# A new token order for the attention quads with an output piece, two DMAs for the rows of maxima, and a second bias that stays in its tile

## The chip, the cores and the metric

The kernel runs on one core of a Trainium2 chip. The metric is device time of one launch in microseconds, here the median of three runs. A profile is one further execution under the hardware profiler, with times of its own.

## The reference

One transformer block on a 2048 x 576 input, all in fp32. A modulation vector comes from silu(c) @ w_mod and gives shifts (sa, sb), scales (ca, cb) and gates (ga, gb). Attention has 32 query heads of width 18 over one shared key and value head; the MLP has 4608 hidden columns.

```python
x = A_x
h = layernorm(x) * (1 + ca) + sa
q = (h @ wq)  # 32 heads of 18
k, v = h @ wk, h @ wv  # one head of 18
p = softmax(q k^T / sqrt(18))
x = x + ga * ((p v) @ wo)
h = layernorm(x) * (1 + cb) + sb
y = layernorm(h)
x = x + gb * (gelu(y @ w1 + b1) @ w2 + b2)
```

## The kernel before

**Stages.** First come the norm, the projections of q, k and v, and the maxima of the first quad. Then attention, which the change is about, and last the MLP, in 36 steps (18 column groups for each half of the rows).

**Attention in quads.** A quad `n` is four heads and one block of 512 rows: 4 blocks x 8 quads = 32 quads (0 to 31). Matmuls of the scores contract over 64 rows of the array: two heads side by side in row group 0 and two in row group 1. A query tile `qst` holds for each group the split query and, in two more rows (`R3`), the negated maximum of every query row, so that the score matmul subtracts it. So the maxima of quad n+1 have to be found while quad n runs.

**The order written out by hand.** PE's work in a quad is a string of tokens (lines 884 to 896), and the loop at line 982 goes through it: `QUAD` for quads 0 to 8, `QUADW` for quads 9 to 30, `LAST` for quad 31. The tokens:

- `S0`, `S1` (`st_mm`, line 928): scores of 128 keys against 512 queries in row group 0 or 1, into one of four `psB` buffers; ACT writes the exponential to `P` (line 934). 64 a quad.
- `M0`, `M1` and `R1` (`mx_mm`, line 938): scores of 128 queries against 512 keys in row group 0 or 1, into one of three `psM` buffers; DVE takes the maximum along each row (line 954). For `R1` it is joined with the result of an earlier `X1` (line 952). `X1` goes through `psB` and is evicted by ACT (line 945). Together 64 a quad.
- `V2`, `V3`, `V4` (`pv_mm`, line 915): so many units of P times V into the single `psC`, 64 units a quad, 8 units behind the scores: the first 8 units in quad n belong to quad n-1. A key block is 4 units. At each full key block, `between` (line 956) puts a step of other work into the queues: at odd ones a step of `fill` (the layer norm of finished output tiles), and from quad 4 on one or two steps of `prep` (splitting and storing the MLP's weights, on POOL, with DMAs on SP's queue), except at the three key blocks in `quiet`.
- `T1`, `RC`, `T2`, `OS`: the steps of `post_quad` (line 733) for quad n-1. ACT copies `psC` to `O` as soon as its last unit is done (line 738); `T1` is a DVE transpose (741), `RC` a DVE reciprocal and a POOL product (744, 745), `T2` a DVE transpose (747), `OS` an ACT copy, a POOL difference and four DMAs (757, 758, 762). There is one `O`.
- `F1`, `F2` (`smax_fin1`, `smax_fin2`, lines 347 and 355): F1 reduces the maxima of quad n+1 on DVE; F2 transposes them on PE (357), ACT and DVE negate and split them into `ms` (359, 360), and SP's queue sends them to the query tile (364).
- `WO` (line 971): one output piece, a 128-row tile by 288 columns of P V @ wo for an earlier block, 14 matmuls into a `psB`, added to the rows by DVE (727). There is one in each quad of `QUADW`. Behind the second piece of a tile in the first two blocks, which falls in the even quads 10 to 24, the layer norm of that tile is put into `fill` (`ln2_rows`, `ln2_tile`): statistics on DVE (143, 147, 148), the norm on POOL (585, 599, 600), statistics again, the norm again, the second bias added (617); its transposes on PE follow the WO two quads later.

An engine runs its own instructions in the order of the program and waits where an operand or a buffer is not ready. A matmul's wait for a PSUM buffer shows at its weight load (PEld).

**The second bias.** `load_b2` and `b2_scaled` (lines 625 and 630) load b2 to all partitions and scale it on POOL by the gate and by 2. This is done once in attention and once more at the start of the MLP, since the tile's pool is closed in between (lines 1100 and 1409).

Of the kernel before, what the change touches and what calls it, by code (L numbers as in the profile page):

```python
# [8 lines left out]
F32 = mybir.dt.float32  # L9
# [15 lines left out]
R3 = 3 * DH  # L25
# [7 lines left out]
def block_kernel(ctx: ExitStack, tc, x, wqkv, wo, w1, b1, w2, b2, c, wmod, ident_in, out):  # L33
# [94 lines left out]
    QST = {}  # L128
# [226 lines left out]
    def smax_fin2(n):  # L355
        p = psB()
        pe.transpose(p[:16, :128], MR.pop(n), ident)  # L357
        ms = pa.tile([16, 2, 128], F32R, name="ms")
        ac.activation(ms[:, 0], p[:16, :128], AF.Copy, scale=-1.0)
        ve.scalar_tensor_tensor(ms[:, 1], p[:16, :128], -1.0, ms[:, 0].bitcast(F32), op0=ALU.mult, op1=ALU.subtract)  # L360
        for g in range(2):
            for s in range(2):
                r = 64 * g + R3 + s
                sy.dma_start(QST[n][r:r + 1].rearrange("o p (t c) -> o (p t) c", c=128).bitcast(F32),
                             ms[8 * g:8 * (g + 1), s].bitcast(F32))


    for t in range(NT):
# [254 lines left out]
        yield  # L623

    def load_b2():
        b2g = px.tile([128, D], F32, name="b2g")
        sy.dma_start(b2g, b2.to_broadcast([128, D]))
        return b2g

# [103 lines left out]
    def post_quad(n, PV):  # L733

        tb, qd = divmod(n, NQ)
        e = po if n < NQT - 1 else ve
        O = px.tile([128, TB], F32, name="O")
        ac.activation(O, PV, AF.Copy)
        yield
        T = px.tile([128, 16, 32], F32, name="T")  # L740
        ve.transpose(T.rearrange("p a b -> p (a b)"), O)
        yield
        R = px.tile([128, 16], F32, name="R", bufs=2)
        ve.reciprocal(R, T[:, :, DH])
        e.tensor_tensor(T, T, R[:, :, None].to_broadcast([128, 16, 32]), op=ALU.mult)
        yield
        ve.transpose(O, T.rearrange("p a b -> p (a b)"))
        yield
        if tb not in ATT:
            assert tb  # L750
            ATT[tb] = big()
        A = ATT[tb].rearrange("p (s k) t -> p s k t", s=2)
        if n == NQT - 1:
            os = A[:, :, KD - 1, :]
        else:
            os = px.tile([128, 2, TB], F32R, name="os")
        ac.activation(os[:, 0], O, AF.Copy)  # L757
        e.tensor_tensor(os[:, 1], O, os[:, 0].bitcast(F32), op=ALU.subtract)  # L758
# [125 lines left out]
    QUAD = """S0 M0 S1 S1 M0 V3 S0 M1 S1 M0 M1 S0 V3 M0 S1 M1 S0 V2 M0 S1 S1 M0 X1 S0 V4 T1 X1 M0 M1 M0 S1 S0
            V4 S1 RC M0 S1 S0 M0 S0 M1 V3 S0 M1 R1 S1 S0 M0 X1 V3 M0 S1 S1 R1 S0 M0 S1 V3 M0 X1 M0 S0 S1 S0
            M1 V3 M0 S1 S1 M0 S0 R1 S0 V3 R1 S0 S1 M1 S0 M0 X1 V3 M0 S1 M0 S1 S0 S0 R1 V3 M0 X1 S0 M1 S0 M1
            V3 S1 M0 M0 S1 T2 S0 S1 V4 M0 S1 S0 M1 S0 M1 V3 S0 R1 S1 M0 F1 S1 S0 V3 X1 M0 S1 M0 R1 S0 F2 OS
            V4 M0 M1 S0 S1 M0 X1 V4 S1 M0 S1 S0 M1 M0 S1 V2 R1 S0 M1 S0 V2 S0 S1 M0 M1 V2 S1""".split()
    QUADW = """M1 M1 S0 S0 X1 S1 M0 V4 S1 M0 S1 S0 M1 M0 V4 M0 S1 S0 M0 S1 T1 M0 X1 V4 S1 RC S0 S0 M1 M0 S1 V4
            S0 R1 M1 S0 S1 M0 S1 V3 S1 M0 S0 X1 M0 M0 S1 V2 M0 S1 S0 R1 V2 M0 X1 M0 S1 S0 S1 M0 V4 S0 T2 R1  # L890
            M0 S1 OS S0 M1 WO S0 R1 M1 S0 M1 S0 X1 V3 S0 M1 M0 S1 S1 M1 S0 V3 M0 S1 S0 R1 S0 M0 X1 V3 M0 S1
            X1 M0 S1 M0 S1 V4 S1 M0 R1 S0 M1 S0 V4 S0 M1 M0 F1 S1 S0 S1 V4 M0 S1 M0 X1 S0 M1 F2 V4 M1 S0 S0
            S1 M0 S1 M0 V3 R1 S0 S0 S1 R1 M0 V3 S0 S1 M0 S1 M0 S1 V3 M0 S1 M1 S0 M1 S0 V3""".split()
    LAST = """S1 S0 S1 S0 V8 S1 S0 T1 S1 S0 RC S1 S0 WO S0 S1 S0 T2 S1 V5 S1 S0 S1 S0 S1 OS S0 V11 S0 S1 S0 S1 S0
            S1 WO RW S1 S0 S0 S1 S0 S1 V8 S0 S1 S0 S1 S0 S1 V8 S1 S0 S1 S0 S0 S1 WP S0 S1 S0 S1 V8 S0 S1 S0 S1
            S0 S1 V8 S0 S1 S0 S1 S0 S1 WP S0 S1 S0 S1 V12""".split()
# [85 lines left out]
    for n in range(NQT):  # L982
# [367 lines left out]
    for v in range(NV):  # L1350
# [158 lines left out]
```

## Time and profile before

| | us |
|---|---|
| median of 3 runs (2224.18 to 2224.81) | 2224.63 |
| the profiled execution | 2227.88 |
| its span, first to last instruction | 2225.8 |
| PE busy | 2204.6 |
| DVE busy | 1931.1 |
| ACT busy | 1639.8 |
| POOL busy | 1524.9 |
| from one F2 transpose to the next, QUADW | 39.3 to 39.9 |

A row of the profile names line and engine, the operation, the tile written and the tiles read, the shapes, the count, then busy time and the mean of one instruction, then the engine's idle time ahead of them and what ended it. A row of a timeline has the start in us from the span's beginning, the time that the merged instructions took from the first start to the last end, engine, line, operation, tiles and count; in brackets the idle time before it. A row of the windows has a stretch, its length, and the busy time (with the count of instructions) of PE, PEld, DVE, ACT and POOL, then the granted clock, the DMA share and GB/s. The granted TensorE clock was 0.997 of full speed over the span. Matmuls overlap in the rows, so starts are more telling than durations.

### The profile page before, as it was taken

What the parts mean: (1) busy time and instruction counts of PE and PEld (TensorE: products, weight loads), DVE (VectorE), ACT (ScalarE), POOL (GpSimd) and SP (SyncE); (2) the same over time, 40 slices, a digit from 0 to 9 for tenths busy, and PEclk for the clock granted to TensorE, in tenths of its full rate; (3) what the DMA queues carried; (4) which work ended last, traced back from release to release, by engine and by line L of the source; (5) the groups of instructions that cost most, each with busy time, mean ns of one, the idle gap of its engine ahead of it and who ended that gap; (6) DMA issues with size and microseconds to landing.
All of it is one profiled execution on the core that took longest, in us unless ns stands there. A gap on an engine that the chain in (4) does not pass through costs nothing.

```text
span 2225.8 us, 46116 instructions
## 1 busy us (share of the span) xinstructions
PE 2204.6 (99%) x16638; PEld 1450.8 (65%) x16638; DVE 1931.1 (87%) x3417; ACT 1639.8 (74%) x3145; POOL 1524.9 (69%) x1761
## 2 busy tenths in 40 slices
PE   8999999999999999999999999999999999999999
PEld 6654545454544545445454446888888898989898
DVE  7589999999999999999999983887888878888887
ACT  5569999999999999999999998544444444343443
POOL 6654356666776687677676640988888867877776
PEclk9999999999999999999999999999999999999999
DMA  6242143343333332333333322666666646676664
GB/s 228 85 133 93 34 128 122 127 137 109 125 121 123 115 129 94 114 130 111 115 121 118 125 70 69 200 179 174 178 179 181 185 129 182 180 218 188 177 184 124
DMA packets 184776, 308.00 MB, mean 138 GB/s; under 512 B 19711, under 2 KB 75407, under 8 KB 184549
## 3 DMA queue, kind: packets, MB, share of 16 engines
q1 hardware_dynamic: 184405, 304.91, 44.2%
q8 instruction: 132, 2.16, 0.4%
q14 instruction: 95, 0.78, 0.1%
q10 hardware_dynamic: 144, 0.15, 0.0%
HBM read 200.97 MB, written 93.79 MB: 132 GB/s over the span
## 4 chain that ended last, share of the span: by engine, by line
PE 92%; ACT 1%; DVE 1%; POOL 0%; issue 0%; DMA 0%; ACTq 0%; POOLq 0%; DVEq 0%
PE psC L922 23%; PE psB L1147 18%; PE psA L1250 16%; PE psB L932 14%; PE psM L319 12%; PE psB L723 2%; PE psB L942 2%; PE psA L1284 1%; ACT P L934 1%; PE psA L723 0%; PE psB L155 0%; PE psB L248 0%; PE psB L357 0%; DVE mx L344 0%; DVE mx L337 0%
## 5 line engine op out<-in xcount | busy, mean ns | idle before, releaser
L934 ACT ACTIVATE P<-psB 128x512 f32<-128x512 f32 x2013 | 1055.0, 620 | 42.7 <-PE psM L319 19.4
L954 DVE TENSOR_REDUCE mx<-psM 128x1 f32<-128x512 f32 x1476 | 934.2, 682 | 30.7 <-PE psM L319 16.0
L932 PE MATMUL psB<-qst,KS 64*128 64x512 f32 x2013 | 606.3, 434 | 0.1
L319 PE MATMUL psM<-KS,qst 64*128 64x512 f32 x1722 | 591.5, 435 | 0.6 <-DVE mx L337 0.5
L922 PE MATMUL psC<-P,V 128*32 128x256 f32 (+3 forms) x6608 | 569.0, 440 | 0.0
L932 PEld LDWEIGHTS psB<-qst,KS 64*128 64x128 f32 x2013 | 302.6, 184 | 218.3 <-ACT P L934 185.5
L319 PEld LDWEIGHTS psM<-KS,qst 64*128 64x128 f32 x1722 | 284.0, 184 | 186.1 <-DVE mx L954 130.5
L1147 PE MATMUL psB<-ops,w1a 128*128 128x512 f32 x1512 | 393.8, 396 | 0.2 <-DVE h L1162 0.2
L1147 PEld LDWEIGHTS psB<-ops,w1a 128*128 128x128 f32 x1512 | 270.1, 188 | 46.6 <-DVE h L1162 0.6
L922 PEld LDWEIGHTS psC<-P,V 128*32 128x32 f32 x6608 | 147.0, 108 | 187.9 <-issue 160.4
L1256 DVE TENSOR_TENSOR XT<-psA,XT 128x576 f32<-128x576 f32 x330 | 241.7, 753 | 20.1 <-PE psA L1250 14.7
L1250 PEld LDWEIGHTS psA<-w2s,big 128*128 128x128 f32 x1584 | 222.9, 188 | 15.5 <-POOL big L1224 3.6
L1250 PE MATMUL psA<-w2s,big 128*128 128x288 f32 x1584 | 230.8, 295 | 0.9 <-POOL big L1224 0.8
L1160 ACT ACTIVATE psB<-gs 128x512 f32<-128x512 f32 x144 | 86.7, 602 | 127.9 <-DVE gs L1159 127.8
L1224 POOL TENSOR_TENSOR big<-s,big 128x512 fp32r<-128x512 f32 x132 | 170.9, 1295 | 10.6
L952 DVE CUSTOM_DVE_ANT_0 xc<-psM,xc 128x512 f32<-128x512 f32 x246 | 166.3, 682 | 12.7 <-PE psB L932 4.5
L1156 ACT ACTIVATE h<-psB,b1t 128x512 f32<-128x512 f32 x144 | 97.9, 680 | 102.0 <-PE psB L1147 79.7
L945 ACT ACTIVATE xc<-psB 128x512 f32<-128x512 f32 x246 | 154.6, 628 | 4.2 <-PE psM L319 1.5
L758 POOL TENSOR_TENSOR os<-O,os 128x512 fp32r<-128x512 f32 x31 | 39.9, 1286 | 171.3 <-ACT os L757 171.3
L1159 DVE SCALAR_TENSOR_TENSOR gs<-psB,h 128x512 f32<-128x512 f32 x144 | 98.5, 684 | 38.5 <-ACT psB L1157 38.3
L792 POOL TENSOR_TENSOR r<-r,r 128x256 fp32r<-128x256 f32 (+1 forms) x162 | 121.8, 752 | 13.0
L1165 ACT ACTIVATE big<-h 128x512 fp32r<-128x512 f32 x39 | 24.7, 633 | 133.8 <-DVE h L1162 133.8
(212 smaller groups left out, 3325.2 us busy)
## 6 DMA issues: line engine op xcount, KB each, us to landing
w1a<-w1scr SPq DMA_DIRECT2D x252, 256.0 KB
w2s<-w2sum SPq DMA_DIRECT2D x132, 288.0 KB
w1scr<-r SPq DMA_DIRECT2D x126, 256.0 KB
w2s<-w2scr SPq DMA_DIRECT2D x76, 288.0 KB
w2scr<-r SPq DMA_DIRECT2D x72, 288.0 KB
w2sum<-r SPq DMA_DIRECT2D x72, 288.0 KB
qst<-qscr SPq DMA_DIRECT2D x192, 72.0 KB
w1a<-w2scr SPq DMA_DIRECT2D x33, 288.0 KB
```

The source lines that it names most:

```text
L319: pe.matmul(o, QST[n][64 * g:64 * g + 64, p, 128 * qt:128 * (qt + 1)], KS[64 * g:64 * g + 64, 512 * kb:512 * (kb + 1)], start=True, stop=True)
L792: po.tensor_tensor(o[:, n:2 * n], src, o[:, :n].bitcast(F32), op=ALU.subtract)
L922: pe.matmul(PVt[n][32 * j:32 * (j + 1), cs], V[:, kc, :], t[:, j, cs], start=(kc == 0 and h0 == 0), stop=(kc == 15), skip_group_check=True)
L932: pe.matmul(t, KS[64 * g:64 * g + 64, 128 * kc:128 * (kc + 1)], QST[n][64 * g:64 * g + 64, i, :], start=True, stop=True)
L934: ac.activation(P[n, kc][:, 2 * i + g, :], t, AF.Exp, scale=SCALE)
L945: ac.activation(XC[-1], t, AF.Relu)
L952: ve.tensor_tensor_reduce(c, t, c, 1.0, -3.0e38, ALU.add, ALU.max, o)
L954: ve.tensor_reduce(o, t, axis=AX.X, op=ALU.max)
L1147: pe.matmul(o, x, y, start=(first and i == 0), stop=(i == len(terms) - 1), skip_group_check=True)
L1224: po.tensor_tensor(unit(u, 1), x, unit(u, 0).bitcast(F32), op=ALU.subtract)
L1250: pe.matmul(p[:, i, :288], x[:, ts_], W2S[k][:, y], start=(bool(first) and q == 0), stop=(q == 2), skip_group_check=True)
L1256: ve.tensor_tensor(o, p[:, :, :288], o, op=ALU.add)
```

## The change

Five edits. `QUAD` is only wrapped anew, its tokens are the same. `QUADW` has the same kinds and numbers of tokens for scores, maxima and steps in another order; the 64 units of P V are cut into one V2, ten V3 and eight V4 in place of two, eight and nine; T1 stands behind unit 19 (was 8), RC behind 28 (12), T2 and WO behind 34 (27), OS behind 61 (27), F1 and F2 both behind 52 (44 and 48). The key blocks in `quiet` follow from the places of F2 and RC; they are 6, 11 and 12 in QUADW (were 2, 10 and 11). The rows of maxima go out in two DMAs of 16 rows rather than four of 8. The second bias has a tile that lives to the end, so the second load and the second scaling go. `post_quad` may step `fill` for the first block's tile, which is there by then anyway.

```diff
-        for g in range(2):
-            for s in range(2):
-                r = 64 * g + R3 + s
-                sy.dma_start(QST[n][r:r + 1].rearrange("o p (t c) -> o (p t) c", c=128).bitcast(F32),
-                             ms[8 * g:8 * (g + 1), s].bitcast(F32))
+        for s in range(2):
+            r = R3 + s
+            sy.dma_start(QST[n][r:r + 65:64].rearrange("g p (t c) -> g (p t) c", c=128).bitcast(F32),
+                         ms[:, s].bitcast(F32))
...
-        b2g = px.tile([128, D], F32, name="b2g")
+        b2g = per.tile([128, D], F32, name="b2g")
...
         if tb not in ATT:
-            assert tb
-            ATT[tb] = big()
+            while not tb and tb not in ATT:
+                step(fill)
+            if tb not in ATT:
+                ATT[tb] = big()
...
-    QUADW = """M1 M1 S0 S0 X1 S1 M0 V4 S1 M0 S1 S0 M1 M0 V4 M0 S1 S0 M0 S1 T1 M0 X1 V4 S1 RC S0 S0 M1 M0 S1 V4
-            S0 R1 M1 S0 S1 M0 S1 V3 S1 M0 S0 X1 M0 M0 S1 V2 M0 S1 S0 R1 V2 M0 X1 M0 S1 S0 S1 M0 V4 S0 T2 R1
-            M0 S1 OS S0 M1 WO S0 R1 M1 S0 M1 S0 X1 V3 S0 M1 M0 S1 S1 M1 S0 V3 M0 S1 S0 R1 S0 M0 X1 V3 M0 S1
-            X1 M0 S1 M0 S1 V4 S1 M0 R1 S0 M1 S0 V4 S0 M1 M0 F1 S1 S0 S1 V4 M0 S1 M0 X1 S0 M1 F2 V4 M1 S0 S0
-            S1 M0 S1 M0 V3 R1 S0 S0 S1 R1 M0 V3 S0 S1 M0 S1 M0 S1 V3 M0 S1 M1 S0 M1 S0 V3""".split()
+    QUADW = """M1 X1 S0 S1 M0 S0 R1 V4 M0 S1 M0 X1 S1 M0 V4 S0 M1 M0 S1 S0 S1 M0 V4 S0 M1 S0 S1 M0 X1 M0 V4 S0 M1
+            M0 S1 S0 S1 M0 V3 R1 S0 S1 R1 S0 M0 T1 S1 V4 S0 S1 M0 M1 M0 S1 V2 X1 S0 S1 M0 V3 RC M0 S1 S0 M1 S0
+            M1 V3 S1 S0 M0 M1 S0 S1 V3 M0 S1 S1 M0 S0 T2 R1 WO X1 M0 M1 M0 X1 S0 S1 V3 R1 S0 S0 M1 S1 M1 S0 V4
+            S0 M1 X1 M0 S1 S0 V3 R1 M0 S1 S0 S1 M0 V4 M0 S1 S0 R1 S0 S1 M0 V4 X1 F1 M0 S1 M0 M1 S0 F2 V3 S1 M0
+            S1 M0 S0 R1 S0 V3 M1 S0 M1 S0 S1 M0 S1 V3 M1 S0 S1 M0 M0 S1 OS V3""".split()
...
-            kf, kr = (sum(int(tok[1]) for tok in order[:order.index(a)] if tok[0] == "V") // 4 for a in ("F2", "RC"))
+            kf, kr = (sum(int(tok[1:]) for tok in order[:order.index(a)] if tok[0] == "V") // 4 for a in ("F2", "RC"))
...
-    B2["b"] = load_b2()
...
-        if v == 0:
-            b2_scaled(B2["b"])
```

More of the change, by code (lines that the diff above doesn't have):

```diff
@@ L883, in block_kernel @@
     LAG = 8
[L884 to L888, printed above, removed]
-    QUADW = """M1 M1 S0 S0 X1 S1 M0 V4 S1 M0 S1 S0 M1 M0 V4 M0 S1 S0 M0 S1 T1 M0 X1 V4 S1 RC S0 S0 M1 M0 S1 V4
-            S0 R1 M1 S0 S1 M0 S1 V3 S1 M0 S0 X1 M0 M0 S1 V2 M0 S1 S0 R1 V2 M0 X1 M0 S1 S0 S1 M0 V4 S0 T2 R1
-            M0 S1 OS S0 M1 WO S0 R1 M1 S0 M1 S0 X1 V3 S0 M1 M0 S1 S1 M1 S0 V3 M0 S1 S0 R1 S0 M0 X1 V3 M0 S1
-            X1 M0 S1 M0 S1 V4 S1 M0 R1 S0 M1 S0 V4 S0 M1 M0 F1 S1 S0 S1 V4 M0 S1 M0 X1 S0 M1 F2 V4 M1 S0 S0
-            S1 M0 S1 M0 V3 R1 S0 S0 S1 R1 M0 V3 S0 S1 M0 S1 M0 S1 V3 M0 S1 M1 S0 M1 S0 V3""".split()
+    QUAD = """S0 M0 S1 S1 M0 V3 S0 M1 S1 M0 M1 S0 V3 M0 S1 M1 S0 V2 M0 S1 S1 M0 X1 S0 V4 T1 X1 M0 M1 M0 S1 S0 V4
+            S1 RC M0 S1 S0 M0 S0 M1 V3 S0 M1 R1 S1 S0 M0 X1 V3 M0 S1 S1 R1 S0 M0 S1 V3 M0 X1 M0 S0 S1 S0 M1 V3
+            M0 S1 S1 M0 S0 R1 S0 V3 R1 S0 S1 M1 S0 M0 X1 V3 M0 S1 M0 S1 S0 S0 R1 V3 M0 X1 S0 M1 S0 M1 V3 S1 M0
+            M0 S1 T2 S0 S1 V4 M0 S1 S0 M1 S0 M1 V3 S0 R1 S1 M0 F1 S1 S0 V3 X1 M0 S1 M0 R1 S0 F2 OS V4 M0 M1 S0
+            S1 M0 X1 V4 S1 M0 S1 S0 M1 M0 S1 V2 R1 S0 M1 S0 V2 S0 S1 M0 M1 V2 S1""".split()
+    QUADW = """M1 X1 S0 S1 M0 S0 R1 V4 M0 S1 M0 X1 S1 M0 V4 S0 M1 M0 S1 S0 S1 M0 V4 S0 M1 S0 S1 M0 X1 M0 V4 S0 M1
[3 more added lines that the diff above has]
+            S1 M0 S0 R1 S0 V3 M1 S0 M1 S0 S1 M0 S1 V3 M1 S0 S1 M0 M0 S1 OS V3""".split()
     LAST = """S1 S0 S1 S0 V8 S1 S0 T1 S1 S0 RC S1 S0 WO S0 S1 S0 T2 S1 V5 S1 S0 S1 S0 S1 OS S0 V11 S0 S1 S0 S1 S0
```

## The prediction

> **What bounds the kernel now.** I read the page first, then the timelines of TensorE (PE), VectorE (DVE), ScalarE (ACT), GpSimd (POOL) and of the DMA queue over single quads, then the windows from one maxima transpose to the next. In the page, see that PE is busy all the time and carries the chain, while its weight loads for the scores stand idle until an ACT or DVE instruction has freed a PSUM buffer.
>
> ```profile
> span 2225.8 us, 46116 instructions
> PE 2204.6 (99%) x16638; PEld 1450.8 (65%) x16638; DVE 1931.1 (87%) x3417; ACT 1639.8 (74%) x3145; POOL 1524.9 (69%) x1761
> PE 92%; ACT 1%; DVE 1%; POOL 0%; issue 0%; DMA 0%; ACTq 0%; POOLq 0%; DVEq 0%
> ...
> L934 ACT ACTIVATE P<-psB 128x512 f32<-128x512 f32 x2013 | 1055.0, 620 | 42.7 <-PE psM L319 19.4
> L954 DVE TENSOR_REDUCE mx<-psM 128x1 f32<-128x512 f32 x1476 | 934.2, 682 | 30.7 <-PE psM L319 16.0
> ...
> L932 PEld LDWEIGHTS psB<-qst,KS 64*128 64x128 f32 x2013 | 302.6, 184 | 218.3 <-ACT P L934 185.5
> ```
>
> The profiled execution took 2227.88 us for its span of 2225.8, 3.25 over the median of 2224.63; the terms below are differences, so I add them to the median.
>
> QUADW rules quads 9 to 30. Quad 30 has no maxima left, so 21 quads count. Their time on PE, by rows (starts are subtracted):
>
> ```profile
> 794.49 0.50 PE L932 MATMUL psB<-qst,KS 64*128 64x512 f32 x2
> ...
> 795.62 1.06 PE L922 MATMUL psC<-P,V 128*32 128x512 f32 x8
> ```
> ```profile
> 808.59 0.50 PE L932 MATMUL psB<-qst,KS 64*128 64x512 f32 x1
> ...
> 809.71 0.86 PE L922 MATMUL psC<-P,V 128*32 128x256 f32 x16
> 810.50 0.50 PE L319 MATMUL psM<-KS,qst 64*128 64x512 f32 x1
> ...
> 820.50 0.49 PE L319 MATMUL psM<-KS,qst 64*128 64x512 f32 x1
> ...
> 821.63 0.85 PE L922 MATMUL psC<-P,V 128*32 128x384 f32 x7
> ```
> ```profile
> 858.19 0.50 PE L319 MATMUL psM<-KS,qst 64*128 64x512 f32 x1
> ...
> 859.09 0.28 PE L357 MATMUL psB<-ident,mxf 128*16 128x128 f32 x1
> 859.29 1.07 PE L922 MATMUL psC<-P,V 128*32 128x512 f32 x8
> 860.29 0.49 PE L319 MATMUL psM<-KS,qst 64*128 64x512 f32 x1
> ...
> 861.50 0.85 PE L922 MATMUL psC<-P,V 128*32 128x384 f32 x8
> ...
> 867.72 0.47 PE L932 MATMUL psB<-qst,KS 64*128 64x512 f32 x1
> ```
>
> Call a run of score and maxima tokens with the V behind it a period. A token of row group 0 and one of row group 1 run together and take one slot; two of one group in a row take two. Three slots took 0.90 us (858.19 to 859.09), four 1.12 (808.59 to 809.71), so 0.22 a slot and 0.68 for two; V3 took 0.79 (809.71 to 810.50), V4 1.00 (859.29 to 860.29), so V2 0.58; the transpose of F2 0.20. A run that takes more than its slots has waited for PSUM: the old fourth period (S1 RC S0 S0 M1 M0 S1, three slots) took 1.13, so 0.23 was lost.
>
> **The change part by part. PE's own work: 0.** Slots by period, old: 4 3 4 3 4 4 2 4 7 4 4 4 3 3 3 4 3 3 3; new: 4 3 4 4 4 4 3 2 3 3 7 4 3 3 4 3 4 4 3 (7 is the run that WO splits into 3 and 4). Both sums are 69, both orders have 19 V with 64 units, and both split one run at WO. What can move is only what PE waits, so I keep a ledger for ACT and for DVE: what a period hands an engine, less the period's length on PE, carried on and never under zero.
>
> **ACT: 0.20 us a quad gained.**
>
> ```profile
> 793.07 1.57 ACT L934 ACTIVATE P<-psB 128x512 f32<-128x512 f32 x3
> 794.50 0.63 ACT L945 ACTIVATE xc<-psB 128x512 f32<-128x512 f32 x1
> ```
>
> Three evictions follow each other in 1.43 us: 0.48 each. The copy of O comes in the third period of both orders; with four evictions that is 2.40 against 2.12, 0.28 behind. Old, the fourth period adds 1.92 against 1.90, and there the 0.23 is lost. New, the fourth is S0 M1 S0 S1 M0 X1 M0: 1.92 against 2.12, and the ledger falls to 0.08. I take 0.20 of the 0.23; the bounds are 0 and 0.23.
>
> **DVE: the new peaks are higher.**
>
> ```profile
> 795.32 0.23 DVE L744 RECIPROCAL R<-T 128x16 f32<-128x16 f32 x1
> ...
> 802.09 1.88 DVE L954 TENSOR_REDUCE mx<-psM 128x1 f32<-128x512 f32 x3
> 803.89 0.45 DVE L147 BATCH_NORM_STATS2 bst<-Z 128x6 f32<-128x288 f32 x1
> 804.38 0.21 DVE L148 BATCH_NORM_AGGREGATE mv<-bst 128x2 f32<-128x12 f32 x1
> 804.50 0.66 DVE L747 STREAM_TRANSPOSE O<-T 128x512 f32<-128x512 f32 x1
> ...
> 818.40 0.19 DVE L352 TENSOR_REDUCE mxf<-mx 128x8 f32<-128x32 f32 x1
> ...
> 820.74 0.27 DVE L360 SCALAR_TENSOR_TENSOR ms<-psB,ms 16x128 fp32r<-16x128 f32 x1
> ```
>
> A maximum costs 0.60 (three from 802.09 to 803.89); R1 I take alike, T1 and T2 0.66 each. F1 has two reductions, by the first 0.19 at most each and partly overlapped: 0.27; F2 0.27. The layer norm of an output tile, which runs in every other pair of quads behind a WO, has statistics of 0.45 and then of 0.61 (803.89 to 804.50).
>
> How much backlog is free, the old order shows. In an even quad the second statistics fall into its 15th period: three maxima, F2 and 0.61 are 2.68 against 0.90+0.20+1.00, a backlog of 0.58, and the run behind it took 1.21 (860.29 to 861.50); in the odd quad without them the same run took 1.13 (820.50 to 821.63). So 0.58 cost 0.08: I count what goes over 0.50, one for one, as lost.
>
> New, in every quad T1 meets two R1 and a maximum (sixth period, R1 S0 S1 R1 S0 M0 T1 S1 V4): 2.46 against 2.12, +0.34; next S0 S1 M0 M1 M0 S1 with only V2 behind it: 1.80 against 1.48. Backlog 0.66, lost 0.16.
>
> In even quads (10, 12 to 24, eight of them) WO stands at unit 34 and no longer at 27, so the statistics come one odd key block later. The first (0.45) fall into the 15th period: 2.25 against 2.12, 0.13. The 16th now holds F1 and F2 together with a V3: 2.34 against 1.89, 0.58. The 17th gives back 0.11; the 18th carries the second statistics: 2.41 against 1.91, 0.97; the 19th: 1.80 against 1.69, 1.08. Over 0.50: 0.58 lost. In the odd quads behind them (eight) that remainder is gone after five periods; the statistics of the normed tile bring the ninth period to about 0.58: 0.08 lost.
>
> **POOL: RC and T2 come close together.**
>
> ```profile
> 799.00 1.05 POOL L745 TENSOR_TENSOR T<-T,R 128x512 f32<-128x512 f32 x1
> ...
> 807.55 1.28 POOL L758 TENSOR_TENSOR os<-O,os 128x512 fp32r<-128x512 f32 x1
> ...
> 828.65 1.95 POOL L135 MEMSET qst<- 32x1024 f32 x2
> ...
> 862.69 2.30 POOL L585 TENSOR_SCALAR Z<-XT,mv,rs 128x576 f32<-128x576 f32 x1
> 865.07 1.42 POOL L599 TENSOR_TENSOR Z<-Z,BC 128x576 f32<-128x576 f32 x1
> ```
> ```profile
> 898.45:938.27 39.82, 39.82 (x350) 19.93 (x348) 37.89 (x76) 37.83 (x77) 23.57 (x34) 1.00 0.34 113
> 938.27:977.66 39.39, 39.39 (x345) 19.06 (x344) 37.99 (x75) 37.33 (x76) 32.78 (x44) 1.00 0.35 114
> ```
>
> The reciprocal of RC ended at 795.55 and POOL's product began at 799.00, 3.45 late, but T2 came at 804.50, so 4.45 were to spare. New, RC stands at unit 28 and T2 at 34: 0.90+0.79+0.90+0.79+0.90 = 4.28, less 0.23 and 1.05, leave POOL 3.0 of lateness. What it has to do since OS, now at unit 61: 1.28, in odd quads the norm (2.30+1.42, and L600 estimated like L599: 5.14), the clearing of a quad's buffer 1.95, and 12 preparation steps at about 0.84 ((23.57-1.05-1.28-1.95)/23, 23 steps a quad in both orders): 18.5, begun 0.6 behind OS (ACT's copy), against 0.79 and eight periods, 16.0. So it is about 3.1 late, just what is free. DVE waits at T2, with R1 and WO's addition queued behind; PE sees it only after the output piece. Bounds 0 and 1.5 an odd quad, the upper one if its waits for stores fall there; I take 0.25, near the computed 0.1.
>
> OS itself moves with a copy on ACT, 1.28 on POOL and four DMAs on SP. Behind them stand preparation stores and the next query loads, which nothing needs within the quad; the rows of maxima are issued before them. The next copy of O, 0.79+2.12+1.90 later, hides POOL's part. Cost 0; if POOL were behind there, ACT would hold psC.
>
> **Two DMAs: 0.**
>
> ```profile
> 860.48 2.84 SPq L364 DMA_DIRECT2D qst<-ms  x4
> ```
>
> Four issues took 2.84 and ended 4.40 before the next quad's first score (867.72). New, that score is 0.20+6.30+0.3 = 6.8 behind F2 and the issues begin 1.39 behind it and take 1.42, or 2.84 if the price goes by rows: 4.0 or 2.6 are left for landing. If landing needs more, every quad pays the rest.
>
> **Second bias: 1.0 us gained, once.**
>
> ```profile
> 1397.95 1.43 POOL L631 TENSOR_TENSOR b2g<-b2g,BC 128x576 f32<-128x576 f32 x1
> 1399.47 1.67 POOL L632 TENSOR_SCALAR b2g<-b2g 128x576 f32<-128x576 f32 x1
> ```
> ```profile
> 1403.33 3.06 PE L1147 MATMUL psB<-ops,w1a 128*128 128x512 f32 x12 [0.19 <-DVE h L1162]
> ...
> 1408.35 1.59 PE L1250 MATMUL psA<-w2s,big 128*128 128x288 f32 x10 [0.81 <-POOL big L1224]
> ```
>
> POOL's two products go, 3.1 us on the way to the GELU sums for which PE waits 0.81, then 0.19 for DVE. Next late would be DVE's h. Bounds 0 and 1.0 in seen waits; I take 1.0. The reload's DMA goes too, off the chain.
>
> **Sum.** Quads 9 and 26 to 29: 5 x (0.16-0.20) = -0.2. Odd: 8 x (0.16+0.08+0.25-0.20) = 2.3. Even: 8 x (0.16+0.58-0.20) = 4.3. Less 1.0: +5.4, so 2230.0 us.
>
> **The rivals. Faster.** PE's three psM buffers may swallow a backlog of 1.0 when it grows over several periods; then the DVE terms fall away and ACT's whole 0.23 is won: 21 x 0.23 + 1.0 = 5.8, 2218.8 us. For it: the loss that a row shows is ACT's. Against it: 1.21 against 1.13 came at a backlog of 0.58. It decides if the runs of the 7th and 19th periods keep 0.90.
>
> **No difference.** PE's waits have one cause in both orders, four psB and three psM buffers, and only the bias pays: 2223.6 us. For it: 218.3 us of idle weight loads spread over all quads. Against it: 1.21 and 1.13 differ with the same buffers. The Trainium skill, Perfetto Trace Analysis, Optimization Strategy, says that the same gap repeating on the engine that should be saturated can mean too few PSUM buffers; by that rule the order alone gives nothing.
>
> **Slower yet.** POOL's stores push its lateness in odd quads to the upper bound, and T2 costs 1.5: 8 x 1.25 more, 2240.0 us. For it: 3.45 late already. Against it: WO covers. A late landing of the maxima I hold for 3 in 100.
>
> **How the numbers follow.** About 0.2%, 4.4 us, is what a measurement here can tell from no change. The forecast's ledger has 0.50: its terms give +1 to +10, of which 0.36 lies over 0.2% and 0.14 under. Faster 0.20, no difference 0.13, slower yet 0.14, landing 0.03. So faster 0.20, same 0.27, slower 0.53. The range 2218 to 2240 ends at the outer rivals.
>
> **What would show it.** Right: unchanged V times, the new fourth run at 1.12, the run before V2 (0.90 bare) and the last runs of even quads longer than their slots, T2 straight behind POOL's product in odd quads. Wrong: quads of 39.3 and 39.9 us or less in place of more, or a first score that waits for a DMA.

## The result and the profile after

The changed kernel takes 2243.84 us (median of 5 runs, 2242.39 to 2245.43), the kernel before, run beside it, 2224.63 (5 runs, 2223.74 to 2227.01). The ratio is 1.0086, with an interval of 1.0074 to 1.0097: 19.2 us slower, where 5.4 were forecast and the range ended at 2240. The profiled execution took 2242.97 for its span of 2241.2.

The page of the kernel after; its lines L935, L955 and L933 are L934, L954 and L932 of before.

```profile
span 2241.2 us, 46379 instructions
PE 2210.4 (99%) x16814; PEld 1457.2 (65%) x16814; DVE 1929.6 (86%) x3417; ACT 1643.0 (73%) x3145; POOL 1523.7 (68%) x1759
PE 87%; DVE 5%; POOL 4%; ACT 1%; issue 1%; DMA 1%; SPq 0%; POOLq 0%; ACTq 0%; DVEq 0%
...
L319 PE MATMUL psM<-KS,qst 64*128 64x512 f32 x1722 | 588.0, 441 | 11.5 <-DVE mx L953 9.9
...
L933 PEld LDWEIGHTS psB<-qst,KS 64*128 64x128 f32 x2013 | 309.1, 185 | 174.3 <-ACT P L935 125.6
L319 PEld LDWEIGHTS psM<-KS,qst 64*128 64x128 f32 x1722 | 272.0, 185 | 209.1 <-DVE mx L955 150.8
```

The busy times hardly moved. The chain did: PE's share fell from 92% to 87%, DVE's rose from 1% to 5% and POOL's from 0% to 4%. The idle weight loads of the scores fell from 218.3 to 174.3 us, so ACT holds PE less; those of the maxima rose from 186.1 to 209.1, so DVE holds it more. And a wait is new: that of L319 as PE itself, not as weight load, idle 9.9 us for DVE at L953, which is R1's maximum.

The windows of the kernel after, one for each quad, from first token to first token: quads 10 to 17, then quad 27. The columns are length, PE, PEld, DVE, ACT, POOL, granted clock, DMA share, GB/s.

```profile
506.97:546.77 39.80, 39.69 (x355) 19.80 (x352) 37.78 (x76) 37.76 (x77) 23.56 (x33) 1.00 0.35 114
546.77:592.28 45.51, 42.36 (x355) 19.99 (x352) 37.66 (x75) 37.24 (x75) 37.66 (x48) 0.92 0.31 105
592.28:632.67 40.39, 40.27 (x361) 20.48 (x357) 38.12 (x77) 38.35 (x78) 21.42 (x33) 1.00 0.34 109
632.67:673.60 40.93, 39.80 (x355) 19.18 (x351) 37.66 (x75) 37.28 (x75) 33.30 (x43) 1.00 0.36 124
673.60:713.99 40.39, 40.27 (x360) 20.50 (x356) 38.09 (x77) 38.34 (x78) 25.17 (x37) 1.00 0.30 98
713.99:753.47 39.48, 39.48 (x355) 19.30 (x351) 37.58 (x75) 37.11 (x75) 35.78 (x47) 1.00 0.39 134
753.47:793.84 40.37, 40.26 (x360) 20.48 (x356) 38.09 (x77) 38.31 (x78) 20.36 (x31) 1.00 0.32 105
793.84:836.11 42.27, 39.84 (x355) 19.22 (x351) 37.68 (x75) 37.29 (x75) 35.75 (x45) 1.00 0.36 118
...
1201.09:1240.23 39.14, 39.14 (x355) 19.50 (x351) 37.06 (x73) 37.36 (x76) 25.41 (x37) 1.00 0.34 113
```

Read three kinds of quads. Quad 27, without a norm, takes 39.14 (39.25 before). The even quads 12 to 24 take 40.38, each like the other (39.91 before), and quad 10, the first, 39.80 (39.36). The odd quads 11 to 25 took 39.27 before, all alike within 0.04; now no two neighbours agree: 45.51, 40.93, 39.48, 42.27, 40.69, 39.49, 43.67 and 39.92, on average 41.50. In quads 11, 13 and 17 PE is busy 1.1 to 3.2 us less than the quad is long, and in quad 11 the granted clock is 0.92. POOL is far busier in odd quads than in even ones, 33 to 38 us against 20 to 25.

The sum of it: quads 9 to 30 took 867.35 us and now take 888.24, so 20.9 more. Eight odd quads give 8 x 2.23 = 17.8 of that, the even ones 3.7, the others -0.7. From quad 31 to the end it was 886.30 and is 885.72. The spans of the two profiles differ by only 15.4, because the profiled execution of before took 4.9 us more ahead of quad 9, where its clock was at half once more (from 48.9 to 52.3). The change has no part in that: the version with the new order alone, up to there the same kernel as before, also took some 4 us less.

Where PE stands in quad 11, in PE's timeline of the kernel after:

```profile
566.76 2.12 PE L722 MATMUL psB<-wos,big 126*128 126x288 f32 x14
568.80 0.50 PE L943 MATMUL psB<-KD,qst 64*128 64x512 f32 x1
568.81 0.72 PE L319 MATMUL psM<-KS,qst 64*128 64x512 f32 x2
572.68 0.79 PE L319 MATMUL psM<-KS,qst 64*128 64x512 f32 x1 [3.15 <-DVE mx L953]
```

After the output piece PE gets two more maxima in and stops: all three psM buffers are full. It waits for R1's buffer, and DVE's and POOL's timelines say why R1 is late.

```profile
562.76 0.24 DVE L743 RECIPROCAL R<-T 128x16 f32<-128x16 f32 x1
...
571.33 0.71 DVE L746 STREAM_TRANSPOSE O<-T 128x512 f32<-128x512 f32 x1 [3.40 <-POOL T L744]
571.96 0.65 DVE L953 CUSTOM_DVE_ANT_0 xc<-psM,xc 128x512 f32<-128x512 f32 x1
```
```profile
543.85 0.23 POOL L149 TENSOR_SCALAR rs<-mv 128x1 f32<-128x1 f32 x1 [10.66 <-DVE mv L148]
...
548.76 1.30 POOL L759 TENSOR_TENSOR os<-O,os 128x512 fp32r<-128x512 f32 x1
550.05 2.31 POOL L584 TENSOR_SCALAR Z<-XT,mv,rs 128x576 f32<-128x576 f32 x1
...
557.39 1.94 POOL L135 MEMSET qst<- 32x1024 f32 x2
...
564.09 1.42 POOL L830 TENSOR_TENSOR w2b<-w2b,BC 128x576 f32<-128x576 f32 x1
...
570.24 1.05 POOL L744 TENSOR_TENSOR T<-T,R 128x512 f32<-128x512 f32 x1
```

The reciprocal ended at 563.00 and POOL's product began at 570.24, 7.2 late, because POOL was still at the work queued ahead of it. T2 waits for the product, and R1 stands behind T2 on DVE. Over the whole execution DVE's wait at T2 comes to 11.2 us in five quads, at most 3.4; the kernel before has no such wait:

```profile
DVE O L746 <- POOL T L744: 11.2, 5, 3.4
```

By the rows of the reciprocal and the product the product is late in quads 11, 13, ... 25 by 7.25, 5.21, 3.50, 6.53, 4.94, 3.58, 6.45 and 3.50. Quads 15 and 21 with about 3.5 are the shortest; above that the quad grows almost one for one: quad 13's product is 1.7 later than quad 15's and the quad takes 1.5 more, quad 17's is 3.0 later and the quad takes 2.8 more. Quad 25, also 3.50 late, takes 39.92, which the lateness does not explain: DVE does not wait at T2 there, but a score's weight load behind the output piece waits 0.51 us for ACT's eviction of an X1, which it does not in quad 21.

### The profile page after: what moved, and what is told of

Its sections match the earlier page's. It is cut to its first block, busy times and chain, and to the rows that moved or that the text cites. A ratio compares the mean times of both kernels' runs of the same rounds, so it can differ in the third digit from the quotient of the medians.

```text
span 2241.2 us, 46379 instructions
## 1 busy us (share of the span) xinstructions
PE 2210.4 (99%) x16814; PEld 1457.2 (65%) x16814; DVE 1929.6 (86%) x3417; ACT 1643.0 (73%) x3145; POOL 1523.7 (68%) x1759
## 4 chain that ended last, share of the span: by engine, by line
PE 87%; DVE 5%; POOL 4%; ACT 1%; issue 1%; DMA 1%; SPq 0%; POOLq 0%; ACTq 0%; DVEq 0%
PE psC L923 20%; PE psB L1147 18%; PE psA L1250 16%; PE psM L319 11%; PE psB L933 11%; PE psB L248 2%; DVE mx L955 2%; PE psB L722 2%; PE psB L943 2%; PE psA L1284 1%; DVE xc L953 1%; POOL r L793 1%; PE psB L155 1%; PE psA L319 1%; PE psA L722 1%
## 5 line engine op out<-in xcount | busy, mean ns | idle before, releaser
L935 ACT ACTIVATE P<-psB 128x512 f32<-128x512 f32 x2013 | 1046.0, 616 | 30.6 <-PE psB L933 12.7
L955 DVE TENSOR_REDUCE mx<-psM 128x1 f32<-128x512 f32 x1476 | 932.1, 682 | 38.0 <-PE psM L319 21.6
L319 PE MATMUL psM<-KS,qst 64*128 64x512 f32 x1722 | 588.0, 441 | 11.5 <-DVE mx L953 9.9
L933 PE MATMUL psB<-qst,KS 64*128 64x512 f32 x2013 | 592.8, 433 | 0.4 <-ACT xc L946 0.2
L923 PE MATMUL psC<-P,V 128*32 128x384 f32 (+3 forms) x6784 | 571.0, 434 | 0.0
L933 PEld LDWEIGHTS psB<-qst,KS 64*128 64x128 f32 x2013 | 309.1, 185 | 174.3 <-ACT P L935 125.6
L319 PEld LDWEIGHTS psM<-KS,qst 64*128 64x128 f32 x1722 | 272.0, 185 | 209.1 <-DVE mx L955 150.8
L923 PEld LDWEIGHTS psC<-P,V 128*32 128x32 f32 x6784 | 153.2, 109 | 195.8 <-issue 167.8
L953 DVE CUSTOM_DVE_ANT_0 xc<-psM,xc 128x512 f32<-128x512 f32 x246 | 166.0, 682 | 20.9 <-PE psM L319 11.8
```

Source lines behind the costliest of these rows:

```text
L319: pe.matmul(o, QST[n][64 * g:64 * g + 64, p, 128 * qt:128 * (qt + 1)], KS[64 * g:64 * g + 64, 512 * kb:512 * (kb + 1)], start=True, stop=True)
L923: pe.matmul(PVt[n][32 * j:32 * (j + 1), cs], V[:, kc, :], t[:, j, cs], start=(kc == 0 and h0 == 0), stop=(kc == 15), skip_group_check=True)
L933: pe.matmul(t, KS[64 * g:64 * g + 64, 128 * kc:128 * (kc + 1)], QST[n][64 * g:64 * g + 64, i, :], start=True, stop=True)
L935: ac.activation(P[n, kc][:, 2 * i + g, :], t, AF.Exp, scale=SCALE)
L953: ve.tensor_tensor_reduce(c, t, c, 1.0, -3.0e38, ALU.add, ALU.max, o)
L955: ve.tensor_reduce(o, t, axis=AX.X, op=ALU.max)
```

## The experiments

**The order alone: the kernel before with the new QUADW and nothing else.**

```diff
-    QUADW = """M1 M1 S0 S0 X1 S1 M0 V4 S1 M0 ...
+    QUADW = """M1 X1 S0 S1 M0 S0 R1 V4 M0 S1 ...
```

> The kernel before with the new QUADW alone (four DMAs for the maxima, the second load of the bias kept). Theory A (the order costs it all, through POOL's late product in odd quads): 19 to 21 us over before, about 2245; odd quads 11 to 25 between 39.5 and 45.5 us as in the changed kernel, even ones 12 to 24 at 40.4. Rival B (the two wider DMAs or the longer-lived bias tile take a part): clearly less, 2230 to 2238.

2246.27 us, ratio 1.010 (1.0085 to 1.0116); odd quads 41.24 on average, even 40.44, light ones 39.16. The whole loss is the order's, and it falls on the odd quads with the same pattern (44.42, 40.94, 39.48, 43.73, ...).

**The rest alone: the kernel after with the old QUADW,** so two DMAs and the bias tile.

```diff
-    QUADW = """M1 X1 S0 S1 M0 S0 R1 V4 M0 S1 ...
+    QUADW = """M1 M1 S0 S0 X1 S1 M0 V4 S1 M0 ...
```

> The changed kernel with the old QUADW put back, so only the two DMAs and the bias tile are left of the change. Theory A (the order costs it all): the quads as before (39.27 odd, 39.91 even), the stretch behind attention 0.6 to 1.0 us shorter for the bias, 2223 to 2224.5. Rival B (the two DMAs or the bias tile cost something that the order's loss hid): 2226 or more.

2223.41 against 2224.45, ratio 0.9994 (0.9985 to 1.0003); odd quads 39.26, even 39.91; from quad 31 on 885.87 where it was 886.30. It is 1.0 us under in the median, as forecast for the bias, but the interval holds 1.

**T2 later: the kernel after, T2 moved by one token run, behind the V3 after the output piece.** POOL's product gets some 3.4 us more (from the reciprocal's end to T2 it is 8.18 in quad 15, where it was 4.83), and nothing else changes. Of the long rows of tokens only the part around the moved one is shown, here and below.

```diff
-... M0 S1 S1 M0 S0 T2 R1 WO X1 M0 M1 M0 X1 S0 S1 V3 R1 S0 S0 M1 ...
+... M0 S1 S1 M0 S0 R1 WO X1 M0 M1 M0 X1 S0 S1 V3 T2 R1 S0 S0 M1 ...
```

> The changed kernel with T2 moved behind the V3 that follows the output piece, so that POOL's product has about 4.7 us more before DVE wants it (slack 3.4 becomes 8). Theory A (what the odd quads lose is DVE waiting at T2 for POOL, one for one beyond the slack, and the TensorE clock that falls behind the longest waits): odd quads fall from a mean of 41.5 to 39.2 to 39.6 us, no half-clock stretch in attention, about 17 us faster than the changed kernel, 2226 to 2228. Even quads stay at 40.4. Rival C (DVE's own backlog from the layer norm statistics in the odd quads): T2 adds 0.66 to another period, odd quads stay over 41 us, 2240 to 2245.

2228.37, ratio 1.0016 (1.0006 to 1.0025): some 15 us of the 19.2 are gone. Odd quads 39.42 to 39.56, even 40.38 and light 39.14 as in the kernel after. Here DVE's and POOL's timelines of quad 11 in this version:

```profile
564.03 0.24 DVE L743 RECIPROCAL R<-T 128x16 f32<-128x16 f32 x1
...
572.60 0.71 DVE L746 STREAM_TRANSPOSE O<-T 128x512 f32<-128x512 f32 x1
```
```profile
571.51 1.05 POOL L744 TENSOR_TENSOR T<-T,R 128x512 f32<-128x512 f32 x1
```

The product is as late as before, 571.51 - 564.27 = 7.2; it is late by 5.23 in quad 13 and 6.51 in quad 17. POOL was not made faster. T2 only stands where nobody needs R1 yet, and starts the moment the product ends, without an idle time of DVE. That the wait at T2 made the loss is shown by this run: the quads in which T2 did not wait, 15 and 21, the even and the light ones, keep their times, so it is not T2's own 0.7 us on DVE. Only quads 9 and 25 gain 0.5 each though T2 had not waited in them.

**The statistics earlier: the kernel after, with one more step of `fill` behind a WO whose transposes are done,** so that statistics and norm come one odd key block earlier.

```diff
             if held[0] == "T":
                 held[0] = step(fill)
+                if held[0] != "T":
+                    step(fill)
```

> The changed kernel with one more step of the fill queue behind the transposes at WO, so that statistics and norm of the next tile come one odd key block earlier (statistics at key blocks 9 and 11, norm at 13 and so ahead of OS on POOL). Theory A with the DVE ledger: the norm's 5.1 us leave the stretch from OS to RC, POOL's product is 0 to 3 us late and T2 does not wait: odd quads 39.2 to 39.6; the second statistics no longer fall behind F1 and F2: even quads 39.8 to 40.0 in place of 40.4; in all 2222 to 2226. Theory A without the ledger (even quads slow for another reason, the place of F1 with F2): even quads stay at 40.4, 2226 to 2229. Rival C': the statistics moved, the odd quads keep over 41 us: 2238 or more.

2234.91, ratio 1.0045 (1.0031 to 1.0059). Odd quads 13 to 23 fall to some 39.7, since POOL's product there is now 1.4 to 2.8 late, so that DVE no longer waits; quad 25 takes 40.18. Even quads fall to 40.11. Quad 11 keeps 45.68: the first tile has a further step (the load of the bias), so its statistics do not move, and its product stays 7.21 late and its clock falls as before; with that quad the total misses the 2222 to 2226 that were expected. So the lateness has a second handle: where POOL's wait for the statistics stands.

**Both together.** The two edits above in one kernel.

```diff
-... M0 S1 S1 M0 S0 T2 R1 WO X1 M0 M1 M0 X1 S0 S1 V3 R1 S0 S0 M1 ...
+... M0 S1 S1 M0 S0 R1 WO X1 M0 M1 M0 X1 S0 S1 V3 T2 R1 S0 S0 M1 ...
...
+                if held[0] != "T":
+                    step(fill)
```

> Both edits: T2 behind the output piece's run and the layer norm one odd key block earlier. Theory A with the ledger: odd quads 39.1 to 39.3, even quads 39.7 to 39.9, quads 26 to 29 at 39.1 as in the changed kernel, so 0.1 us a quad under before: 2220 to 2224. If the longer order of steps costs elsewhere (the transpose of T2 in the period with R1): 2224 to 2228.

2227.83, ratio 1.0014 (1.0005 to 1.0023); odd 39.69, even 40.11, light 39.14. Against before that is +0.42, +0.20 and -0.11 a quad. The statistics moved their cost from even to odd quads, where the 9th run takes 1.50 (0.93 in light quads).

**A filler for PE: the kernel after, with 14 further matmuls of 128x128 ahead of the third maximum behind WO in quads 11, 17 and 23.** Their result is not used; the rest is computed as in the kernel after.

```diff
+        if n in (11, 17, 23):
+            order = list(order)
+            order.insert(order.index("WO") + 4, "W")
...
+            if tok == "W":
+                p = psB()
+                for _ in range(14):
+                    pe.matmul(p[:, :128], ident, ident, start=True, stop=True)
```

> The changed kernel with 14 extra 128-column matmuls (about 3.1 us, their result is not used) ahead of the third maximum behind WO in quads 11, 17 and 23 alone, where PE waits some 3 us for DVE. Theory E (part of the loss in these quads is the TensorE clock that falls to half behind a long idle wait): no half-clock stretch in attention; quads 11, 17 and 23 take 39.3 plus what POOL is late beyond 3.4 us, about 43.0, 42.3 and 42.3, in place of 44.4 to 45.5, 42.3 to 43.7 and 42.2 to 43.7. Rival F (the wait alone costs it all): the same times as without the filler, or up to 3 us more where it does not fit into the wait.

One run: 2240.12, beside 2224.16 for before. The windows of quad 11 over the wait and behind it, first in the kernel after, then here:

```profile
568.80:572.70 3.90, 0.75 (x6) 0.31 (x5) 1.37 (x4) 0.60 (x1) 3.74 (x7) 0.90 0.37 131
572.70:579.00 6.30, 6.30 (x45) 3.02 (x45) 3.99 (x8) 3.64 (x7) 5.97 (x8) 0.52 0.25 94
```
```profile
569.58:573.55 3.97, 3.97 (x32) 3.49 (x31) 1.45 (x4) 0.60 (x1) 3.81 (x7) 1.00 0.30 105
573.55:579.83 6.28, 6.28 (x64) 3.31 (x63) 5.45 (x11) 5.67 (x12) 5.95 (x8) 1.00 0.26 97
```

In the kernel after PE stands for most of 3.9 us, and then runs 6.3 us at a granted clock of 0.52 on average, in which it gets 45 matmuls done. With the filler it is busy throughout, the clock stays at 1.00, and as long a stretch holds 64. The product is as late as before (7.26), and the quad takes 42.98 in place of 45.51 although PE has 3.4 us more to do. Quad 17, where the kernel after had kept its clock, takes 0.7 more with the filler (42.97); quad 23 takes 0.7 less (42.99). The times without half clock that theory E gave are met in quad 11 and exceeded by 0.7 in the other two, by the filler itself. So the half clock is a loss of its own behind the wait: 2.5 us or more in quad 11. This is one run, without an interval; the quads agree with each other.

**T1 earlier.** From here on, DVE tokens are moved to test the ledger, which holds that only a period's sum matters. First T1 into the fourth period, ahead of its last maximum, on top of both shifts:

```diff
-... V4 S0 M1 S0 S1 M0 X1 M0 V4 S0 M1 M0 S1 S0 S1 M0 V3 R1 S0 S1 R1 S0 M0 T1 S1 V4 ...
+... V4 S0 M1 S0 S1 M0 T1 X1 M0 V4 S0 M1 M0 S1 S0 S1 M0 V3 R1 S0 S1 R1 S0 M0 S1 V4 ...
```

> T2 late, the norm early, and T1 moved from the sixth to the fourth period (behind unit 12), where DVE has 0.3 us to spare. DVE ledger: the backlog of 0.66 ahead of the ninth period is gone, so in odd quads the ninth run falls from 1.50 to about 1.0: odd quads 39.69 to 39.2, the others 0.05 less, even quads 40.05: 4 to 5 us under the two edits alone, 2223 to 2224. Rival D (the ninth run in odd quads is long because the reciprocal of RC or the statistics wait for POOL's norm, not from a backlog): odd quads stay at 39.6 to 39.7, 2227 to 2228.

2232.48, ratio 1.0035 (1.0021 to 1.0049): slower than with both shifts alone, in every kind of quad (40.04, 40.28, 39.30). The fifth run went from 1.12 to 1.38 in all of them. The ninth run in odd quads fell as the ledger wanted, but from 1.50 to 1.38 and not to 1.0. DVE's and PEld's timelines of quad 27 in this version:

```profile
1196.88 0.68 DVE L955 TENSOR_REDUCE mx<-psM 128x1 f32<-128x512 f32 x1
1197.48 0.70 DVE L740 STREAM_TRANSPOSE T<-O 128x512 f32<-128x512 f32 x1
1198.10 1.85 DVE L955 TENSOR_REDUCE mx<-psM 128x1 f32<-128x512 f32 x3
```
```profile
1198.81 0.18 PEld L319 LDWEIGHTS psM<-KS,qst 64*128 64x128 f32 x1 [0.24 <-DVE mx L955]
```

The weight load at 1198.81 is for the run's second M0, which needs the buffer of the third maximum before it. That one's reduction is the first of the three from 1198.10, and stands behind T1's transpose.

**T1 and F1 earlier,** F1 behind the first M0 of the run before its own, on top of that.

```diff
-... V4 M0 S1 S0 R1 S0 S1 M0 V4 X1 F1 M0 S1 M0 M1 S0 F2 V3 ...
+... V4 M0 F1 S1 S0 R1 S0 S1 M0 V4 X1 M0 S1 M0 M1 S0 F2 V3 ...
```

> The same and F1 put one period ahead of F2 (behind the 24th M0, its last operand). DVE ledger with F2 waiting for F1: in even quads the run with F2 falls from 1.42 to 1.11 or 1.15: even quads 39.75 to 39.85, odd 39.2, light 39.05 to 39.1: 2220 to 2222.5, 0.1 to 0.2% under before. If PE's transpose did not wait for F1, even quads stay at 40.05: 2223 to 2224.

2236.65, ratio 1.0055 (1.0042 to 1.0067): slower again, and F2's run grew, to 1.72 in even quads.

**The same without the earlier statistics.**

```diff
-                if held[0] != "T":
-                    step(fill)
```

> T2 late, T1 and F1 early, but the layer norm at the changed kernel's key blocks (second statistics at 13, norm at 15). Theory A: T2 has its slack, so POOL's norm between OS and RC does no harm: odd quads 39.1 to 39.2. DVE ledger: even quads keep the last run at 1.4 (second statistics, 0.47 lost) but not the run with F2: 40.05 to 40.1. In all 2222.5 to 2224.5.

2235.61, ratio 1.0052 (1.0038 to 1.0065); odd 39.71, even 40.87, light 39.45. The loss does not hang on the statistics' place.

**T1 behind its run's last maximum,** in place of ahead of it, on top of both shifts.

```diff
-... V4 S0 M1 S0 S1 M0 X1 M0 V4 S0 M1 M0 S1 S0 S1 M0 V3 R1 S0 S1 R1 S0 M0 T1 S1 V4 ...
+... V4 S0 M1 S0 S1 M0 X1 M0 T1 V4 S0 M1 M0 S1 S0 S1 M0 V3 R1 S0 S1 R1 S0 M0 S1 V4 ...
```

> As e6 (T2 late, norm early, T1 in the fourth period), but T1 stands behind that run's last maximum and no longer ahead of it, so DVE does the transpose under the V4. Theory G (what counts is not the sum of DVE's work in a period but whether it stands ahead of an eviction that the next run's maxima wait for): the fifth run falls from 1.38 to 1.12, every quad 0.26 less than in e6: light 39.05, odd 39.7, even 40.0, about 2225 to 2227. Rival H (the sums decide, as in the ledger): the fifth run stays at 1.38, 2232.

2230.99, ratio 1.0031 (1.0019 to 1.0043), where 2225 to 2227 were expected. The fifth run is back at 1.12, as theory G has it, but the sixth went from 1.17 to 1.27, and to 1.63 in odd quads, where statistics follow T1 on DVE.

**F1 behind its new run's last maximum as well.**

```diff
-... V4 M0 S1 S0 R1 S0 S1 M0 V4 X1 F1 M0 S1 M0 M1 S0 F2 V3 ...
+... V4 M0 S1 S0 R1 S0 S1 M0 F1 V4 X1 M0 S1 M0 M1 S0 F2 V3 ...
```

> As e10 with F1 behind the last maximum of the run before F2, under its V4. Theory G: F2's run does not get longer by it, as it did in e7 (1.22 light, 1.72 even); in even quads, where PE's transpose waits for F1 behind the statistics, it falls from 1.42 to 1.1 to 1.2, light and odd keep 1.0 and 1.1: even quads 39.75, about 2223 to 2225. Rival H: no change against e10 or longer.

2230.74, ratio 1.0029 (1.0018 to 1.0041). F1's place changed nothing: F2's run in even quads takes 1.42, as with both shifts alone, where theory G expected 1.1 to 1.2. The rows of both shifts alone say why: in quad 14 the run's third maximum waits 0.42 us at its weight load for a reduction that stands behind the statistics on DVE, and then the transpose waits 0.24 us for ACT's eviction of an X1. It does not wait for F1.

**RC behind its run's last maximum,** on top of both shifts.

```diff
-... RC M0 S1 S0 M1 S0 M1 V3 S1 S0 M0 M1 S0 S1 V3 ...
+... M0 S1 S0 M1 S0 M1 RC V3 S1 S0 M0 M1 S0 S1 V3 ...
```

> The version with both shifts (T2 behind the period that follows the output piece, statistics one odd key block earlier) has a median of 2227.83 and odd quads of 39.69, and in the 9th period of its odd quads the run takes 1.50 where light quads take 0.93: the second statistics (0.45 and 0.21) and the reciprocal of RC (0.24) all stand on DVE ahead of the maxima whose buffers the run needs. Here RC alone moves, behind the last maximum of the same run; no work leaves the period. A ledger by periods says: the same backlog, so no change, 2227.8, odd run 1.50. The view by places in the queue (a run waits only for what stands on DVE ahead of the third maximum before) says: the odd run shortens by about the reciprocal, to 1.25, the others to 0.89, so 8 x 0.25 + 13 x 0.04, some 2.5 us: 2225.3, if the next run (0.89 in odd quads) does not take the wait over. T2 now stands a whole period later, so POOL's product, which starts about 0.9 later, should hold nothing.

2228.4, ratio 1.0017 (1.0008 to 1.0026), odd 39.68, and the 9th run of odd quads 1.51: no change, as the ledger said. The view by places was applied wrongly in the expectation, and the rows show where. DVE's timeline of quad 15, first with both shifts, then with RC moved, and PE's with both shifts:

```profile
720.36 1.85 DVE L955 TENSOR_REDUCE mx<-psM 128x1 f32<-128x512 f32 x3
722.13 0.44 DVE L147 BATCH_NORM_STATS2 bst<-Z 128x6 f32<-128x288 f32 x1
722.60 0.21 DVE L148 BATCH_NORM_AGGREGATE mv<-bst 128x2 f32<-128x12 f32 x1
722.73 0.64 DVE L955 TENSOR_REDUCE mx<-psM 128x1 f32<-128x512 f32 x1
723.28 0.24 DVE L743 RECIPROCAL R<-T 128x16 f32<-128x16 f32 x1
```
```profile
722.72 0.21 DVE L148 BATCH_NORM_AGGREGATE mv<-bst 128x2 f32<-128x12 f32 x1
722.85 2.43 DVE L955 TENSOR_REDUCE mx<-psM 128x1 f32<-128x512 f32 x4
725.19 0.24 DVE L743 RECIPROCAL R<-T 128x16 f32<-128x16 f32 x1
```
```profile
722.91 0.39 PE L933 MATMUL psB<-qst,KS 64*128 64x512 f32 x1
723.42 0.49 PE L319 MATMUL psM<-KS,qst 64*128 64x512 f32 x1
```

The maximum at 723.42 is the run's third. It waits for the buffer of the maximum ahead of this run, whose reduction runs from 722.73 to 723.37. Ahead of that stand the statistics, not the reciprocal, which comes behind it in either order. Moving the reciprocal could bring nothing here; by this reading, which no run here tests, moving the statistics would.

No version with the new order, as it is or with tokens moved, beats the kernel before. The only version under it in the median is the old order with the other two edits.

## Why the prediction was wrong

**The step that failed** is "POOL: RC and T2 come close together". It named the engine, the tokens and the wait, and that PE would see it only after the output piece; all of that is what the timelines show. It took 0.25 us an odd quad for it, between 0 and 1.5. Measured against the version with T2 later, it is (41.50 - 39.47) = 2.03 on average, 16.2 us over the eight odd quads; 1.5 is exceeded in three of them. DVE's waits at T2 come to 11.2 us, and the half clock, below, adds 4 or more.

Three of its numbers were off. What is free was taken too low, 3.0 where it is 3.8: DVE waited at T2 for 3.40 us in quad 11, where the product was 7.25 late, and for 1.37 in quad 13, where it was 5.21 late. That error by itself would have made the loss smaller. Wrong the other way was "begun 0.6 behind OS". ACT's copy for OS began at 546.62 ahead of quad 11 and POOL's difference at 548.76, 2.1 behind; in quad 13 it is 632.51 and 635.23, 2.7 behind. In an even quad POOL's queue holds the wait for the second statistics (the row with 10.66), and six instructions of weight preparation stand behind that wait and ahead of OS (4.1 us of them ahead of quad 11). The prediction moved those statistics to a later key block in its DVE ledger, and did not follow them to POOL, where POOL's waits for them grew:

```profile
POOL rs L149 <- DVE mv L148: 49.1, 17, 5.4
```
```profile
POOL rs L149 <- DVE mv L148: 97.7, 10, 14.7
```

These are the rows of the waits of the kernel before and of the kernel after: us in total, times, longest. Wrong too was an average price for steps that differ. From OS to the product POOL took 18.84 in quad 13, as computed (18.5), but 21.48 in quad 11, where the stretch holds the tail of one weight and two products of 1.42 (L830). So the lateness is 3.5 to 7.3 by the stretch of preparation that a quad happens to meet. Where the sum stands at the edge of what is free, the spread decides, and not the mean. The other term of the odd quads was low too: with T2 later they still take 0.33 more than the light ones, and it stands in their ninth run, 1.30 for three slots, where the ledger lost 0.08.

**What the prediction did not have** is the clock. In quad 11 it fell to half for 6.8 us, from 2.35 us into PE's wait on; in quad 23 for 3.4 us, from 0.85 us behind the wait on. Quad 23 took 43.67 with it and 42.16 in the order-alone version without it; quad 17 took 42.27 without it and 43.73 there with it, so 3.4 us at half clock cost 1.5. Why it falls in one quad and not in another is in the last section.

**The rivals.** "Slower yet" had the price, 2240.0, and the place, T2, but for another cause: there is no wait for a store on POOL from 548.76 to 570.24. "Faster" fell, "no difference" too: the version with the old order shows that the same buffers with another order make 20 us. The rule quoted there from the Trainium skill, Perfetto Trace Analysis, Optimization Strategy, does not tell these cases apart.

**Even quads:** 0.54 forecast, 0.47 measured. The size is right, and its cause in part: with the statistics one odd key block earlier 0.27 of it is gone. **Light quads:** -0.04 forecast, -0.12 measured in quads 27 to 29; quad 9, which the forecast counts with them, took some 0.45 more, and no longer with T2 later. ACT's gain of 0.20 is there: the old fourth run's 1.13 for three slots gave way to 1.12 to 1.17 for four. But DVE's 0.16 "in every quad" is not: the run before V2, which was to be longer than 0.90, takes 0.89. The ledger was wrong there in kind. DVE's sum over a period does not say whether PE waits. By the rows, PE waits when something stands on DVE ahead of the reduction of the third maximum before. In the new order T1 stands where three maxima later nobody waits; a period earlier it costs 0.26. The rows of the runs with T1 earlier and with RC moved show this in two places, and those of F2's run in a third; the ledger's 0.50 of free backlog is not a constant of the kernel. As a forecast this view did no better: the versions with T1 behind, F1 behind and RC behind all missed the time that it gave them. So it is a reading of rows, and no run has won time by it. That both shifts together still stay 3.4 us over the kernel before is read, in the odd quads, off the 9th run and the statistics in the rows above; no experiment moved them out of it, and in the even quads, with 0.20, off F2's run as said above.

**Two DMAs:** 0 forecast. SP's row of the kernel after:

```profile
586.95 1.34 SPq L363 DMA_DIRECT2D qst<-ms  x2
```

Two issues take 1.34, about as much each as the four before (2.84), and no first score of a quad waited for them. **Second bias:** 1.0 forecast once, 0.6 from quad 31 on and 1.0 in the median of the version with the old order; its interval, 0.9985 to 1.0003, does not tell that from nothing. Of the two waits of PE that were to go, 0.81 for POOL is gone and the one for DVE is still there:

```profile
1419.99 3.07 PE L1147 MATMUL psB<-ops,w1a 128*128 128x512 f32 x12 [0.20 <-DVE h L1162]
...
1423.37 1.75 PE L1250 MATMUL psA<-w2s,big 128*128 128x288 f32 x12
```

## What to carry to other kernels

Where a consumer's place in a hand-written order comes close to its producer, work the producer's lateness out for the worst stretch of its queue, with what stands ahead of it behind a wait of its own; an average over the whole quad hides it. Follow every moved step to all engines that wait for it, here the statistics from DVE to POOL. With a pool of n buffers, ask of each side instruction whether it stands ahead of the eviction of the n-th buffer before the one that is needed; a sum per period does not answer that. Then follow the wait on, since a moved instruction can hold the next run in place of this one.

## What the hardware showed that was not expected

A stall of PE of two to three us inside a busy stretch can halve its clock afterwards. In the kernel after, PE's idle before R1's release was 3.15 in quad 11, and the clock was at half for 6.8 us; 2.37 in quad 23, and half for 3.4 us; 2.43 in quad 17, and not at all. In the order-alone version the same wait of 2.44 in quad 17 was followed by 3.4 us at half clock. So it does not go by the length alone.

The traces' records of the granted clock show what it goes by. The two falls in the kernel after, at 571.88 and 1063.40 us, lie 144 times 3.413 us apart, and those of the order-alone version, at 574.05 and 819.81, 72 times. So there is a grid of 3.413 us that runs on whatever the kernel does. The windows of that grid in the kernel after, the one before the fall of quad 23 and then the two over quad 17's wait (columns as above):

```profile
1059.98:1063.40 3.42, 1.05 (x9) 0.53 (x12) 2.21 (x6) 0.87 (x2) 3.25 (x7) 1.00 0.25 86
814.23:817.64 3.41, 2.37 (x16) 1.77 (x15) 0.75 (x2) 1.60 (x4) 3.27 (x6) 1.00 0.31 106
817.64:821.05 3.41, 2.02 (x24) 1.28 (x25) 3.38 (x7) 1.45 (x3) 3.14 (x6) 1.00 0.20 78
```

Quad 23's wait falls into one window, which leaves PE 1.05 us of work there; quad 17's is split between two, which keep 2.37 and 2.02. In the five falls of quads 11, 17 and 23 in the kernel after, the order-alone version and the one with earlier statistics, the window before had 0.49 to 1.06 us of work; the windows over the two waits without a fall had 2.01 to 2.50. The fall lasted two windows where the wait reached into the first of them, and one where it did not. Whether a wait of 2.4 us costs 1.5 us more is thus luck: it hangs on where the grid lies.

The Trainium skill, TensorE: Matmul & The Clock Gate, Part 1, says that the clock falls to half after an idle window of some 3.4 us and that the window runs freely. The grid agrees with that. That the window need not be idle throughout is more than the page says: PE worked for up to 1.06 us of it and the clock fell all the same. Where between 1.06 and 2.01 us of work the border lies, no run here shows.
